# Attention and gated convolution on one core: row-tiled bf16 transposes for q and k, whole-head copies out of PSUM, and a last product split by rows

## The chip, the cores and the metric

The kernel runs on 1 core of one Trainium2 chip. The metric is the device time of one execution in microseconds (us).

PE is the matmul engine (TensorE), DVE is VectorE, ACT is ScalarE, POOL is GpSimd, SP issues DMAs. In this program PE, DVE and ACT each have a fixed order of instructions, so one that is late holds up those behind it (PE's wait of 3.45 us below is such a case).

## The reference, cut to what matters

```python
# q, k, v: (8 batches, 8 heads, 576 positions, 64), float32
scores = (q @ k.T) / 8, kept only where |i - j| <= 32
attn   = softmax(scores);  x = attn @ v, heads side by side: (8, 576, 512)
h      = relu(x @ w_in)                      # 512 -> 1024
conv   = three taps along the sequence, one weight per channel
out    = (h * sigmoid(conv)) @ w_out         # 1024 -> 512
```

Inputs and output are float32; the kernel computes in bf16. Scores are small (q and k are drawn with 0.1 deviation), so the weights within a window are nearly equal.

## The kernel before: the parts that matter

The kernel writes no instruction order by hand. A planner in Python takes operations with estimated costs, priorities and buffers, plays them on a model of the engines, and emits the result as a fixed order per engine. So each change of a cost, a buffer count or a rule may reorder the whole program.

q and k arrive with the head dimension along the free axis, and the scores need it on the partitions. A partition holds 9 neighbouring positions, so a turned row has position `r * 9 + j` (r: partition, j: 0 to 8). Nine 128x128 matmuls against the identity turn one pair of heads, and copies put the results in order:

```python
for n, js in enumerate(((0, 1, 2, 3), (4, 5, 6, 7), (8,))):
    ...
    tensor.matmul(ps.ap[:, x:x + 128], h.ap[:, j]..., ident, start=True, stop=True)   # float32 in PSUM
    ...
    if n < 2:                                  # 512 elements, written in runs of 4, 18 bytes apart
        o_ = to.ap[:, 2*y:2*y+2, PAD:PAD+S].rearrange("p x (r j) -> p x r j", j=RP)
        copier(e, o_[:, :, :, js[0]:js[0]+4], ps.ap.rearrange("p (j x r) -> p x r j", j=4, x=2))
if y == 1:                                     # j = 8 of q and k: 256 single elements, 18 bytes apart
    copier(e, o_[:, :, :, RP - 1], cs.ap[:, 0:256].rearrange("p (x r) -> p x r", x=4))
```

The middle tap of the convolution runs on PE for chunk 0 and on DVE for the others (`TAP(c, m): c > 0`), w_out is cast by POOL or DVE (`ENG1`), and the products with w_out come last in a chunk:

```python
def project(c, i, prio):                       # 12 chunks of 384 rows, 3 blocks of 128 rows each
    ...
    for m in range(MB):                        # 8 row blocks of w_out, one accumulation
        tensor.matmul(ps.ap, gT.ap[:, m, 128*i:128*i+128], w_out_sb[:, m, :], start=(m == 0), stop=(m == MB-1))
...
NHT = 4                                        # buffers for the convolution's input, per shape
NRING, NATTN, NGT, NQKB = 4, 3, 3, 8           # loads, weights of attention, gates, staged q and k
AHEAD = 2                                      # PSUM banks that attention must leave free
```

The softmax here doesn't subtract the row's maximum and nothing guards it: scores larger than these inputs give would overflow.

## Time and profile before

| | before |
|---|---|
| time, median of 3 | 273.63 us (271.94 to 273.75) |
| span of the profile | 268.6 us |
| PE / DVE / ACT busy | 89% / 82% / 77% |

These lines are from the profile's page: span, busy time by engine, PE's busy tenths and granted clock in 40 slices of 6.7 us (a 9 is 90% or more), and the chain of work that ended last, by engine.

```profile
span 268.6 us, 6936 instructions
PE 238.9 (89%) x2661; PEld 146.7 (55%) x2686; DVE 221.0 (82%) x522; ACT 206.3 (77%) x465; POOL 55.8 (21%) x80
PE   8799984669799899979999989979999999999974
PEclk9999998668999999999999999999999999999998
PE 49%; DVE 26%; ACT 19%; issue 4%; ACTq 0%; DVEq 0%
```

PE has a hole in the seventh to ninth slice, where the granted clock falls too. The chain is PE for only half of the span and runs through DVE and ACT for 45% of it. That is not all waiting time of PE, which is idle for 11% of the span. The windows view says what was busy around the hole (the first line names the columns; a figure in brackets is the number of instructions, and the last three are granted clock, DMA share and GB/s):

```profile
core 0: us, PE busy (x) PEld busy (x) DVE busy (x) ACT busy (x) POOL busy (x), PEclk, DMA share, GB/s
0.00:40.00 40.00, 34.97 (x440) 24.85 (x441) 33.38 (x108) 32.48 (x74) 4.71 (x26) 1.00 1.00 289
40.00:60.00 20.00, 11.78 (x153) 7.39 (x154) 18.37 (x44) 10.71 (x38) 8.97 (x9) 0.72 0.78 212
60.00:150.00 90.00, 83.34 (x989) 51.83 (x998) 79.48 (x176) 72.98 (x165) 33.00 (x36) 0.99 0.79 220
150.00:245.00 95.00, 90.50 (x992) 53.64 (x1002) 79.01 (x176) 78.44 (x166) 9.12 (x9) 1.00 0.17 53
```

From 40 to 60 us DVE is the busy one. Its timeline (start, duration, engine, operation, out<-in, count) shows four casts of w_out in one block, with the taps that PE needs behind them:

```profile
41.88 1.02 DVE L292 SCALAR_TENSOR_TENSOR gT<-tn,hT 128x384 bf16<-128x384 f32 x2
42.81 3.32 DVE L292 CAST w_out_sb<-st 128x512 bf16<-128x512 f32 x4
46.05 0.24 DVE L292 RECIPROCAL rec<-pf 128x4 f32<-128x4 f32 x2
46.21 0.38 DVE L292 SCALAR_TENSOR_TENSOR tn<-hT,conv_w_sb,pf 128x192 f32<-128x192 bf16 x1
```

PE's timeline of the same microseconds (in brackets the idle time before, and what ended it):

```profile
42.36 0.83 PE L292 MATMUL pf<-hT,diag_w 128*128 128x192 bf16 x8
46.64 1.34 PE L292 MATMUL pf<-qkT 64*128 64x64 bf16 x36 [3.45 <-DVE tn L292]
```

The copies of the turned q and k, from the groups by shape (busy us, mean ns of one, idle before):

```profile
L292 ACT CAST qkT<-pf 128x512 bf16<-128x512 f32 x45 | 33.2, 785 | 2.0 <-PE pf L292 2.0
L292 ACT CAST qkT<-pf 128x256 bf16<-128x256 f32 x13 | 17.7, 1359 | 0.0
L292 DVE CAST qkT<-pf 128x512 bf16<-128x512 f32 x19 | 13.6, 721 | 0.4 <-PE pf L292 0.3
L292 DVE CAST qkT<-pf 128x256 bf16<-128x256 f32 x3 | 3.9, 1294 | 0.0
```

Half as many elements take nearly twice as long in the 256-element form: the difference is how they are written. And PE's last matmuls, from its timeline; the last gate ends on DVE at 261.0 us:

```profile
258.33 0.49 PE L292 MATMUL pf<-hT,diag_w 128*128 128x384 bf16 x2 [0.74 <-ACT hT L292]
258.66 1.67 PE L292 MATMUL pf<-w_out_sb,gT 128*128 128x512 bf16 x6
261.07 3.84 PE L292 MATMUL pf<-w_out_sb,gT 128*128 128x512 bf16 x17 [0.74 <-DVE gT L292]
```

### The profile page before, as it was taken

The page shows a single profiled execution, that of the slowest core. Times are in us where ns is not written, and L with a number is a line of the kernel's source. Part 1 is how long each engine was busy: PE and PEld are TensorE (multiplying, and loading weights), DVE is VectorE, ACT ScalarE, POOL GpSimd, SP SyncE. Part 2 cuts the span into 40 slices and gives each one's busy share as a digit, 9 for nine tenths or more (in the row PEclk, how much of TensorE's full clock was granted, in tenths as well). Part 3 has the DMA queues.
Part 4 walks back from the last instruction along what each step waited for, and adds up shares of the span by engine and source line. Part 5 has one row for each costly group of instructions (what it writes and reads, how often), then busy time and mean ns, then how long its engine had stood idle before and what let it go on. Part 6 is the DMA issues. An engine that isn't in the chain of part 4 may idle for free.

```text
span 268.6 us, 6936 instructions
## 1 busy us (share of the span) xinstructions
PE 238.9 (89%) x2661; PEld 146.7 (55%) x2686; DVE 221.0 (82%) x522; ACT 206.3 (77%) x465; POOL 55.8 (21%) x80
## 2 busy tenths in 40 slices
PE   8799984669799899979999989979999999999974
PEld 5468653248565564454565655555656545655531
DVE  7998599976999988989798986987799878976640
ACT  3898994466796988796877998897787995776642
POOL 2002005601554535063021560130000000000000
PEclk9999998668999999999999999999999999999998
DMA  7999999654995999599911901101202111111213
GB/s 227 265 307 393 246 291 348 113 159 130 292 274 174 261 330 250 159 338 251 297 68 41 220 36 64 56 2 40 82 2 78 41 39 41 41 61 58 79 40 117
DMA packets 53573, 42.40 MB, mean 158 GB/s; under 512 B 38668, under 2 KB 38692, under 8 KB 53540
## 3 DMA queue, kind: packets, MB, share of 16 engines
q1 hardware_dynamic: 53504, 41.95, 54.4%
q8 instruction: 21, 0.34, 0.5%
q14 instruction: 12, 0.10, 0.1%
q10 hardware_dynamic: 36, 0.01, 0.1%
HBM read 32.52 MB, written 9.44 MB: 156 GB/s over the span
## 4 chain that ended last, share of the span: by engine, by line
PE 49%; DVE 26%; ACT 19%; issue 4%; ACTq 0%; DVEq 0%
PE pf L292 49%; ACT qkT L292 7%; DVE gT L292 6%; ACT tn L292 5%; DVE tn L292 4%; DVE attn L292 3%; ACT attn L292 3%; ACT hT L292 3%; DVE xn L292 2%; DVE qkT L292 2%; DVE w_out_sb L292 2%; DVE vo L292 2%; ACT xT L292 1%; DVE ve L292 1%; ACT y L292 1%
## 5 line engine op out<-in xcount | busy, mean ns | idle before, releaser
L292 PE MATMUL pf<-xT,w_in_sb 128*128 128x385 bf16 (+2 forms) x416 | 75.4, 316 | 1.7 <-ACT xT L292 1.0
L292 DVE SCALAR_TENSOR_TENSOR gT<-tn,hT 128x384 bf16<-128x384 f32 (+1 forms) x104 | 58.2, 577 | 15.9 <-ACT tn L292 14.9
L292 PE MATMUL pf<-w_out_sb,gT 128*128 128x512 bf16 x263 | 68.4, 393 | 2.8 <-DVE gT L292 0.7
L292 ACT ACTIVATE tn<-tn 128x384 f32<-128x384 f32 (+1 forms) x96 | 47.8, 523 | 20.1 <-DVE tn L292 19.7
L292 DVE SCALAR_TENSOR_TENSOR tn<-hT,conv_w_sb,pf 128x384 f32<-128x384 bf16 (+1 forms) x96 | 53.3, 575 | 10.4 <-PE pf L292 9.7
L292 ACT ACTIVATE hT<-pf 128x385 bf16<-128x385 f32 (+2 forms) x104 | 50.6, 521 | 8.9 <-PE pf L292 7.9
L292 PEld LDWEIGHTS <-w_in_sb 128*128 128x128 bf16 x416 | 38.9, 98 | 23.5 <-issue 2.2
L292 ACT CAST qkT<-pf 128x512 bf16<-128x512 f32 (+1 forms) x58 | 48.2, 914 | 2.0 <-PE pf L292 2.0
L292 PE MATMUL pf<-hT,diag_w 128*128 128x384 bf16 (+1 forms) x216 | 45.7, 315 | 4.3 <-ACT hT L292 3.1
L292 PEld LDWEIGHTS <-gT 128*128 128x128 bf16 x288 | 28.4, 100 | 33.2 <-issue 4.0
L292 ACT ACTIVATE attn<-pf 128x512 bf16<-128x512 f32 (+1 forms) x96 | 41.1, 538 | 0.4 <-PE pf L292 0.4
L292 POOL TENSOR_SCALAR qkb<-st 128x1152 bf16<-128x1152 f32 x24 | 31.1, 1300 | 46.4 <-DMA st<-in_q_dram 21.7
L292 ACT COPY y<-pf 128x512 f32<-128x512 f32 x35 | 20.8, 594 | 17.4 <-PE pf L292 17.3
L292 POOL TENSOR_SCALAR ve<-vst 128x512 bf16<-128x512 f32 x31 | 20.7, 687 | 49.9 <-PE pf L292 35.7
L292 DVE TENSOR_TENSOR attn<-attn,mask 128x1152 bf16<-128x1152 bf16 x32 | 25.7, 803 | 3.1 <-ACT attn L292 2.8
L292 DVE TENSOR_TENSOR xn<-pf,rec 128x256 bf16<-128x256 f32 x71 | 26.4, 410 | 0.2
L292 PEld LDWEIGHTS <-diag_w 128*128 128x128 bf16 x216 | 18.0, 97 | 14.8 <-issue 5.6
L292 PE MATMUL pf<-ident,qkb 128*128 128x128 bf16 x288 | 24.1, 222 | 2.1 <-DVE qkb L292 1.7
L292 PEld LDWEIGHTS <-qkb 128*128 128x128 bf16 x288 | 18.9, 99 | 7.0 <-DVE qkb L292 2.7
L292 PEld LDWEIGHTS <-qkT 64*128 64x128 bf16 x576 | 11.7, 96 | 17.0 <-issue 12.7
L292 PE MATMUL pf<-qkT 64*128 64x64 bf16 x576 | 15.1, 194 | 6.5 <-DVE tn L292 3.5
L292 PE MATMUL pf<-ve,attn 128*64 128x65 bf16 x384 | 17.2, 198 | 3.7 <-DVE attn L292 3.0
(43 smaller groups left out, 191.0 us busy)
## 6 DMA issues: line engine op xcount, KB each, us to landing
st<-in_q_dram SPq DMA_DIRECT2D x16, 576.0 KB, 6.1
st<-in_k_dram SPq DMA_DIRECT2D x16, 576.0 KB, 6.3
out_dram<-y SPq DMA_DIRECT2D x36, 256.0 KB, 2.0
vst<-in_v_dram SPq DMA_DIRECT2D x24, 256.0 KB, 8.1
vst<-in_v_dram SPq DMA_DIRECT2D x16, 192.0 KB, 4.6
st<-in_moe_w_in_dram SPq DMA_DIRECT2D x2, 1024.0 KB, 7.9
st<-in_moe_w_out_dram SPq DMA_DIRECT2D x2, 1024.0 KB, 7.9
conv_w<-in_moe_conv_w_dram ACTq DMA_DIRECT2D x1, 12.0 KB
```

Source lines behind the costliest of these rows:

```text
L292: return lambda *args, **kwargs: fixed(do(*args, **kwargs))
```

## The change

The intent: let two transposes run side by side in PE's two row halves, keep the turned values in bf16 so that a head's 576 positions fit one PSUM bank, copy a head out in one contiguous write, take load off DVE, and leave PE little to do after the last gate. The fit rests on what the Trainium skill states in "PSUM — Partial Sum Buffer", Specifications: a bank holds 2 KiB per partition, and a transpose writes its input's type while other matmuls write float32 (576 values are 1,152 bytes in bf16 and 2,304 in float32).

The core of the diff; cuts are marked with `...`, and what follows a `#` or stands in brackets is a note:

```diff
-    pf = Pool([psum.tile([128, 512], FP32, name=f"pf{i}") for i in range(8)])
+    pf = Banks(psum.tile([128, 4096], FP32, name="pf"))          # another choice among free banks
 ...
-        for n, js in enumerate(((0, 1, 2, 3), (4, 5, 6, 7), (8,))):
 ...  (the transposes and copies shown above)
+        turned = lambda x: ps[x].ap.bitcast(BF16)[:, 0:S]
+        for n, js in enumerate(((0, 1, 2, 3), (4, 5, 6, 7, 8))):
+            def emit(e, js=js):
+                for j in js:
+                    for x in range(2):
+                        tensor.transpose(
+                            turned(x)[:, 64 * j:64 * j + 64],
+                            h.ap[64 * x:64 * x + 64, j].rearrange("p e d -> p (e d)"),
+                            ident[64 * x:64 * x + 64, 64 * x:64 * x + 64],
+                        )
 ...
+            copier(e, to.ap[:, 2 * y + x, PAD:PAD + S].rearrange("p (r j) -> p r j", j=RP),
+                   turned(x).rearrange("p (j r) -> p r j", j=RP))
 ...
-    return c > 0
+    return c > TAP0                                               # TAP0 = 1
 ...
-    (tap: PSUM -> SBUF tile tn, tanh in place)
+    (tap: in place in PSUM, tanh PSUM -> tn)
 ...
-                cast_w("out", m, CASTWO + 0.1 * m, ENG1)           # POOL, DVE
+                cast_w("out", m, CASTWO + 0.1 * m, ENGW)           # POOL, ACT
 ...
+        cuts = (0, 3, 5, 6, 7, MB) if c == NCH - 1 else (0, MB)   # one operation per cut
-                project(c, i, 8.0 * (c + 1) + (PYAT[i] if c < NCH - 1 else 0.0))
+                project(c, i, 8.0 * (c + 1) + PYAT[i] if c < NCH - 1 else 8.0 * c + 3.6 + 0.1 * i)
 ...
-NHT = 4
-NRING, NATTN, NGT, NQKB = 4, 3, 3, 8
-AHEAD = 2
+NHT = 6
+NRING, NATTN, NGT, NQKB = 4, 3, 2, 6                              # and 5 tn, 3 y buffers
+AHEAD = 0
 ...
-        engines = ("SP", "PE", "ACT", "DVE", "POOL")
+        engines = ("SP", "PE", "POOL", "ACT", "DVE")              # who picks first, in the planner
 ...  (a blocked DVE or POOL operation no longer blocks those behind it, in the planner)
```

More of the change, by code (lines that the diff above doesn't have):

```diff
@@ L22, in __init__, with take, room, give @@
         self.free = [(-1.0, i) for i in range(len(bufs))]
+    def take(self, span):
+        if not self.free:
+            return None
+        self.free.sort()
+        return self.free.pop(0)[1]
+    def room(self, spans, spare):
+        return len(self.free) >= len(spans) + spare
+    def give(self, now, index, span):
+        self.free.append((now, index))
+    def ap(self, index, span):
+        return self.bufs[index]
+class Banks:
+    def __init__(self, tile_):
+        self.tile = tile_
+        self.free = {i: -1.0 for i in range(8)}
+    def runs(self, span):
+        return [i for i in range(9 - span) if all(i + k in self.free for k in range(span))]
+    def take(self, span):
+        if span == 1:
+            at = min(self.free, key=lambda i: (i < 3, self.free[i], -i))
+        else:
+            at = self.runs(span)[0]
+        for k in range(span):
+            del self.free[at + k]
+        return at
+    def room(self, spans, spare):
+        if len(self.free) < sum(spans) + spare:
+            return False
+        return all(s == 1 or self.runs(s) for s in spans)
+    def give(self, now, index, span):
+        for k in range(span):
+            self.free[index + k] = now
+    def ap(self, index, span):
+        return self.tile[:, 512 * index:512 * (index + span)]
 class Slot:
-    def __init__(self, pool):
-        self.pool, self.index, self.users = pool, None, 0
+    def __init__(self, pool, span=1):
+        self.pool, self.span, self.index, self.users = pool, span, None, 0
     @property
     def ap(self):
-        return self.pool.bufs[self.index]
+        return self.pool.ap(self.index, self.span)
 class Op:
@@ L87, in run @@
         mode = None
-        lock = {"DVE": 0.0, "POOL": 0.0}
+        lock = {"DVE": 0.0, "POOL": 0.0, "PE": 0.0}
         dma_free, rings = 0.0, []
@@ L121, in note @@
                 t, d = t + max(x, 1e-6), d - max(x, 1e-6)
-        late[0].free = [x for x in late[0].free if x[1] != late[1]]
+        late.take(1)
         push(filler_until, "free", late)
@@ L143, in run @@
                 elif kind == "free":
-                    x[0].free.append((now, x[1]))
+                    x.give(now, 7, 1)
                 elif kind == "done":
@@ L148, in run @@
                         if not s.users:
-                            s.pool.free.append((now, s.index))
+                            s.pool.give(now, s.index, s.span)
                     for n in x.after:
@@ L158, in run @@
                 while free[e] <= now + 1e-9:
-                    best = None
+                    best, blocked = None, False
+                    other = {"DVE": "POOL", "POOL": "DVE"}.get(e, "PE")
                     for o in todo[e]:
@@ L162, in run @@
                             continue
-                        short = False
+                        if o.two and lock[other] > now + 1e-9:
+                            blocked = True
+                            continue
                         need = {}
                         for s in o.acquire:
-                            need[s.pool] = need.get(s.pool, 0) + 1
-                        for p, n in need.items():
-                            if len(p.free) < n + (o.spare if p is self.psum else 0):
-                                short = True
-                        if short:
+                            need.setdefault(s.pool, []).append(s.span)
+                        if not all(p.room(n, o.spare if p is self.psum else 0) for p, n in need.items()):
                             continue
@@ L178, in run @@
                     if best is None:
+                        if blocked:
+                            free[e] = lock[other]
+                            push(free[e], "look", e)
                         if e == "PE" and now < filler_until:
@@ L187, in run @@
                     t = now
-                    if e in lock and o.two:
-                        other = "POOL" if e == "DVE" else "DVE"
-                        if lock[other] > now + 1e-9:
-                            free[e] = lock[other]
-                            push(free[e], "look", e)
-                            break
                     gone.add(o)
@@ L196, in run @@
                     for s in o.acquire:
-                        s.pool.free.sort()
-                        s.index = s.pool.free.pop(0)[1]
+                        s.index = s.pool.take(s.span)
                     out.append((t, len(out), e, o))
@@ L224, in run @@
                         free[e] = now + occ
-                        if e in lock and o.two:
+                        if o.two and e in lock:
                             lock[e] = now + occ
@@ L228, in run @@
                     push(free[e], "look", e)
+                    o.fin = done
                     push(done + self.LATENCY[e if e == "SP" else "ACT"], "done", o)
@@ L236 @@
 FILL = 23.0
-NHT = 4
-NRING, NATTN, NGT, NQKB = 4, 3, 3, 8
+NHT = 6
+NTN, NQKT, NY = 5, 3, 3
+NRING, NATTN, NGT, NQKB = 4, 3, 2, 6
 LOADV1, LOADWO, CASTWO = -89.0, -89.5, 6.0
+TN_SBUF = True
+MASKER = ("DVE",)
+ENGW = ("POOL", "ACT")
 ENG1 = ("POOL", "DVE")
-AHEAD = 2
+TAP0 = 1
+AHEAD = 0
 PLACE = {0: (-30.0, -10.0), 1: (1.0, 9.0), 2: (11.0, 21.0), 3: (21.0, 31.0), 4: (34.0, 46.0),
@@ L304 @@
     qkb = pool("qkb", NQKB, [128, RP, 2, 64], BF16)
-    qkT = pool("qkT", 3, [128, 4, W], BF16)
+    qkT = pool("qkT", NQKT, [128, 4, W], BF16)
     ve_b = [sb.tile([128, NBLK, H, 65], BF16, name=f"ve{i}") for i in range(2)]
@@ L313 @@
     gT_p = pool("gT", NGT, [128, MB, CH], BF16)
-    tn_p = pool("tn", 4, [128, CH], FP32)
-    y_p = pool("y", 4, [128, d_model], FP32)
+    tn_p = pool("tn", NTN, [128, CH], FP32) if TN_SBUF else None
+    y_p = pool("y", NY, [128, d_model], FP32)
     w_in_sb = sb.tile([128, KC, d_ff], BF16, name="w_in_sb")
@@ L378, with masker @@
     op = pl.op
+    def masker(b):
+        costs = {"DVE": c_dve(1152, 2.0), "POOL": c_pool(1152, 2.6)}
+        return {e: costs[e] for e in (("DVE",) if b < 2 else MASKER)}
     def copier(e, out_, in_):
@@ L507, in transposes @@
             qkT_slot[b, i] = Slot(qkT)
-            c_slot[b, i] = Slot(pf)
-        to, cs = qkT_slot[b, i], c_slot[b, i]
+        to, ps = qkT_slot[b, i], [Slot(pf), Slot(pf)]
         parts = 2 if ("qkb", b, i, y, 1) in pl.writer else 1
-        for n, js in enumerate(((0, 1, 2, 3), (4, 5, 6, 7), (8,))):
-            ps = cs if n == 2 else Slot(pf)
-            reads = [("qkb", b, i, y, 0)] if n == 0 or parts == 1 else [("qkb", b, i, y, 1)]
-            def emit(e, js=js, n=n, ps=ps):
-                for z, j in enumerate(js):
-                    x = 128 * z + (128 * y if n == 2 else 0)
-                    tensor.matmul(
-                        ps.ap[:, x:x + 128], h.ap[:, j].rearrange("p e d -> p (e d)"),
-                        ident, start=True, stop=True,
-                    )
-            first = y == 0 and n == 0
-            acq = ([ps] if n < 2 or y == 0 else []) + ([to] if first else [])
-            o = op(f"tr {'qk'[y]}{b}{i}.{n}", {"PE": 0.0575 * len(js)}, emit, prio, reads=reads + ["ident"],
-                   writes=[("ptr", b, i, y, n)], acquire=acq, behind=None if first else leader["tr", b, i, n == 2],
-                   use=[h] + ([ps] if n == 2 else []), spare=ahead)
-            if first:
-                leader["tr", b, i, False] = leader["tr", b, i, True] = o
-            elif n == 2 and y == 0:
-                leader["tr", b, i, True] = o
-            if n < 2:
-                def emit(e, js=js, ps=ps):
-                    o_ = to.ap[:, 2 * y:2 * y + 2, PAD:PAD + S].rearrange("p x (r j) -> p x r j", j=RP)
-                    copier(e, o_[:, :, :, js[0]:js[0] + 4],
-                           ps.ap.rearrange("p (j x r) -> p x r j", j=4, x=2))
-                op(f"ev {'qk'[y]}{b}{i}.{n}", evac_cost(512), emit, prio + 0.05, reads=[("ptr", b, i, y, n)],
-                   writes=[("qkT", b, i, y, n)], use=[ps, to])
@@ L538, in transposes @@
-        if y == 1:
-            def emit(e):
-                o_ = to.ap[:, :, PAD:PAD + S].rearrange("p x (r j) -> p x r j", j=RP)
-                copier(e, o_[:, :, :, RP - 1], cs.ap[:, 0:256].rearrange("p (x r) -> p x r", x=4))
-            op(f"ev 8{b}{i}", evac_cost(256), emit, prio + 0.05, reads=[("ptr", b, i, y, 2) for y in range(2)],
-               writes=[("qkT", b, i, 2)], use=[cs, to])
+        turned = lambda x: ps[x].ap.bitcast(BF16)[:, 0:S]
[8 more added lines that the diff above has]
+                        )
+            o = op(f"tr {'qk'[y]}{b}{i}.{n}", {"PE": 0.03 * len(js)}, emit, prio, mode="row",
+                   reads=[("qkb", b, i, y, min(n, parts - 1)), "ident"], writes=[("ptr", b, i, y, n)],
+                   acquire=(ps if n == 0 else []) + ([to] if y + n == 0 else []),
+                   behind=leader.get(("tr", b, i, y)), use=[h] + ps, spare=ahead)
+            leader["tr", b, i, y] = o
@@ new lines, in transposes, with emit_ev @@
+        if y == 0:
+            leader["tr", b, i, 1] = o
+        def emit_ev(e, x):
+            copier(e, to.ap[:, 2 * y + x, PAD:PAD + S].rearrange("p (r j) -> p r j", j=RP),
+                   turned(x).rearrange("p (j r) -> p r j", j=RP))
+        for x in range(2):
+            op(f"ev {'qk'[y]}{b}{i}.{x}", evac_cost(S), lambda e, x=x: emit_ev(e, x),
+               prio + 0.05, reads=[("ptr", b, i, y, n) for n in range(2)], writes=[("qkT", b, i, y, x)],
+               use=[ps[x], to])
@@ L551, in scores @@
         for x in range(2):
-            tiles = [Slot(pf), Slot(pf), Slot(pf)]
+            ps = [Slot(pf), Slot(pf), Slot(pf)]
             lists = [[(x, e, t) for t in range(8)] for e in range(2)]
@@ L558, in scores, with emit @@
                     todo += lists[e][n:n + 1]
-            def emit(e_, x=x, tiles=tiles, todo=todo):
+            def emit(e_, x=x, ps=ps, todo=todo):
                 for x_, e, t in todo:
@@ L563, in emit @@
                     tensor.matmul(
-                        tiles[n // 512].ap[:, n % 512:n % 512 + 64],
+                        ps[n // 512].ap[:, n % 512:n % 512 + 64],
                         to.ap[64 * e:64 * e + 64, 2 + x_, 64 * t:64 * t + 128],
@@ L570, in scores, with emit_exp @@
                f"sc {b}{i}{x}", {"PE": 0.28}, emit, prio + 0.001 * x, mode="row",
-               reads=[("qkT", b, i, y, n) for y in range(2) for n in range(2)] + [("qkT", b, i, 2)],
+               reads=[("qkT", b, i, y, x0) for y in range(2) for x0 in range(2)],
                behind=leader["sc", b, i, 0] if x else None,
-               writes=[("sc", b, i, x)], acquire=tiles + ([at_] if x == 0 else []),
+               writes=[("sc", b, i, x)], acquire=ps + ([at_] if x == 0 else []),
                use=[to], spare=ahead)
-            for e in range(3):
-                n = (512, 512, 128)[e]
-                c0 = 1152 * x + 512 * e
-                def emit_exp(e_, e=e, n=n, c0=c0, tiles=tiles):
-                    scalar.activation(at_.ap[:, c0:c0 + n], tiles[e].ap[:, 0:n], AF.Exp, bias=0.0, scale=scale)
-                op(f"exp {b}{i}{x}{e}", {"ACT": c_act(n)}, emit_exp, prio + 0.1,
-                   reads=[("sc", b, i, x)], writes=[("exp", b, i, x, e)], use=[tiles[e], at_])
+            for n, (c0, c1) in enumerate(((0, 512), (512, 1024), (1024, 1152))):
+                def emit_exp(e_, x=x, c0=c0, c1=c1, ps=ps[n]):
+                    scalar.activation(
+                        at_.ap[:, 1152 * x + c0:1152 * x + c1], ps.ap[:, 0:c1 - c0], AF.Exp, bias=0.0, scale=scale
+                    )
+                op(f"exp {b}{i}{x}{n}", {"ACT": c_act(c1 - c0)}, emit_exp, prio + 0.1,
+                   reads=[("sc", b, i, x)], writes=[("exp", b, i, x, n)], use=[ps[n], at_])
             def emit_mask(e_, x=x):
-                vector.tensor_tensor(
+                (vector if e_ == "DVE" else gpsimd).tensor_tensor(
                     out=at_.ap[:, 1152 * x:1152 * x + 1152], in0=at_.ap[:, 1152 * x:1152 * x + 1152],
@@ L589, in emit_mask @@
                 )
-            op(f"mask {b}{i}{x}", {"DVE": c_dve(1152, 2.0)}, emit_mask, prio + 0.15, two=True,
-               reads=[("exp", b, i, x, e) for e in range(3)], writes=[("attn", b, i, x)], use=[at_])
+            op(f"mask {b}{i}{x}", masker(b), emit_mask, prio + 0.15, two=True,
+               reads=[("exp", b, i, x, n) for n in range(3)], writes=[("attn", b, i, x)], use=[at_])
     def values(b, i, c, prio, ahead, engines):
@@ L677, in unit @@
         touched = sorted({(s // S, s % S // 128) for s in range(lo, hi)})
-        ps, pc, tn = Slot(pf), Slot(pf), Slot(tn_p)
+        ps, pc = Slot(pf), Slot(pf)
         hT = Slot(hT_p[shape])
@@ L730, in emit_tap, with emit_tanh @@
                 vector.scalar_tensor_tensor(
-                    out=in3(tn.ap), in0=taps(1), scalar=conv_w_sb[:, 1, m:m + 1], in1=in3(pc.ap),
+                    out=in3(pc.ap), in0=taps(1), scalar=conv_w_sb[:, 1, m:m + 1], in1=in3(pc.ap),
                     op0=ALU.mult, op1=ALU.add,
                 )
-            op(f"tap {u}", {"DVE": c_dve(nc_)}, emit_tap, prio + 0.55, reads=[("pc", u), "conv_w"], writes=[("tap", u)],
-               acquire=[tn], use=[pc, hT])
-            def emit_tanh(e_):
-                scalar.activation(tn.ap[:, 0:nc_], tn.ap[:, 0:nc_], AF.Tanh, bias=0.0, scale=1.0)
-            op(f"tanh {u}", {"ACT": c_act(nc_, sbuf=True)}, emit_tanh, prio + 0.6, reads=[("tap", u)],
-               writes=[("tanh", u)], use=[tn])
-        else:
-            def emit_tanh(e_):
-                scalar.activation(tn.ap[:, 0:nc_], pc.ap[:, 0:nc_], AF.Tanh, bias=0.0, scale=1.0)
-            op(f"tanh {u}", {"ACT": c_act(nc_)}, emit_tanh, prio + 0.6, reads=[("pc", u)],
-               writes=[("tanh", u)], acquire=[tn], use=[pc])
+            op(f"tap {u}", {"DVE": c_dve(nc_ + 58)}, emit_tap, prio + 0.55, reads=[("pc", u), "conv_w"], writes=[("tap", u)],
+               use=[pc, hT])
+        tn = Slot(tn_p) if TN_SBUF else pc
+        def emit_tanh(e_):
+            scalar.activation(tn.ap[:, 0:nc_], pc.ap[:, 0:nc_], AF.Tanh, bias=0.0, scale=1.0)
+        op(f"tanh {u}", {"ACT": c_act(nc_)}, emit_tanh, prio + 0.6, reads=[("tap" if on_dve else "pc", u)],
+           writes=[("tanh", u)], use=[pc], acquire=[tn] if TN_SBUF else [])
         def emit_gate(e_):
@@ L753, in unit @@
         op(f"gate {u}", {"DVE": c_dve(nc_)}, emit_gate, prio + 0.7, reads=[("tanh", u)], writes=[("g", c, m, part)],
-           use=[tn, hT, gT], two=True)
+           use=[tn, hT, gT], two=TN_SBUF)
     out_rows = out.rearrange("b s f -> (b s) f")
@@ L760, in project, with emit @@
         parts = [p for p in (None, 0, 1) if ("g", c, 0, p) in pl.writer]
-        def emit(e_):
-            for m in range(MB):
-                tensor.matmul(
-                    ps.ap, gT.ap[:, m, 128 * i:128 * i + 128], w_out_sb[:, m, :], start=(m == 0), stop=(m == MB - 1),
-                )
         if len(parts) == 2:
             parts = [0] if 128 * i + 128 <= HW else [1] if 128 * i >= HW else parts
-        op(f"py {c}{i}", {"PE": MB * 0.2158}, emit, prio, acquire=[ps], use=[gT], writes=[("py", c, i)],
-           reads=[("g", c, m, p) for m in range(MB) for p in parts] + [("w_out", m) for m in range(MB)])
+        cuts = (0, 3, 5, 6, 7, MB) if c == NCH - 1 else (0, MB)
+        for n, (m0, m1) in enumerate(zip(cuts, cuts[1:])):
+            def emit(e_, m0=m0, m1=m1):
+                for m in range(m0, m1):
+                    tensor.matmul(
+                        ps.ap, gT.ap[:, m, 128 * i:128 * i + 128], w_out_sb[:, m, :],
+                        start=(m == 0), stop=(m == MB - 1),
+                    )
+            leader["py", c, i] = op(
+                f"py {c}{i}.{n}", {"PE": (m1 - m0) * 0.2158}, emit, prio + (n if c == NCH - 1 else 0),
+                acquire=[ps] if n == 0 else [], use=[gT, ps], writes=[("py", c, i, n)],
+                behind=leader.get(("py", c, i)),
+                reads=[("g", c, m, p) for m in range(m0, m1) for p in parts] + [("w_out", m) for m in range(m0, m1)])
         def emit_y(e_):
             copier(e_, y_sb.ap, ps.ap)
-        op(f"y {c}{i}", evac_cost(d_model), emit_y, prio + 0.2, reads=[("py", c, i)], writes=[("y", c, i)],
+        op(f"y {c}{i}", evac_cost(d_model), emit_y, prio + 0.2, reads=[("py", c, i, n) for n in range(len(cuts) - 1)],
+           writes=[("y", c, i)],
            acquire=[y_sb], use=[ps])
@@ L864 @@
             for i in range(3):
-                project(c, i, 8.0 * (c + 1) + (PYAT[i] if c < NCH - 1 else 0.0))
-    order = pl.run(START, (0.107, "filler"), FILL, (pf, 7))
+                project(c, i, 8.0 * (c + 1) + PYAT[i] if c < NCH - 1 else 8.0 * c + 3.6 + 0.1 * i)
+    order = pl.run(START, (0.107, "filler"), FILL, pf)
     order.sort(key=lambda x: (x[0], x[1]))
-    dummy = pf.bufs[7]
+    dummy = pf.ap(7, 1)
     for t, _, e, o in order:
```

## The prediction

> **What bounds it now.** The page gives PE 89% busy, DVE 82%, ACT 77%; the chain that ended last is PE 49%, DVE 26%, ACT 19%. The timeline's starts tell more of PE: a 512-column product takes 216 ns from start to start, a 385-column one 164, a 128x128 transpose 56, a row-tiled 64-column score about 17. Over all matmuls that is about 205 of 268.6 us (estimate). The rest: 118 mode changes (a full matmul before a row-tiled one takes 259 instead of 164 ns: about 12 us), half clock (7 us), waits (some 30 us). The worst stage is 40 to 60 us: in the windows view PE is busy 11.8 of 20 us, DVE 18.4, granted clock 0.72. DVE's timeline shows four w_out casts in one block of 3.3 us, taps behind them, and PE's longest wait (3.5 us, on DVE's tap). From 60 us on PE is mostly 93 to 99% busy.
>
> **What changes.**
> - Transposes: 288 of 56 ns (16.1 us) become 576 row-tiled ones of 64 columns, shaped like the scores: 17 ns each, 10 us. But mode changes go from 118 to 158: +4 us. The Trainium skill, "TensorEngine Tiling (Array Packing)", Key Properties, says that changing the tiling mode drains the array; this trace's 0.1 us agrees. Chunk 1's third tap adds 1.3 us. PE's work hardly falls.
> - Copies out: now 80, ACT 45x785 + 13x1359 ns = 50.9 us, DVE 17.5. The 1359 ns form has 256 elements but writes single ones with gaps: gaps cost. Afterwards 64 copies of 576, written contiguously. Contiguous xT copies of 512 took 631 (ACT) and 685 ns (DVE), so about 690 and 750: ACT 35 -> 24 us, DVE 29 -> 22.
> - DVE also loses w_out casts (4.4), chunk 1 taps (6.4), casts of q, k, v, w_in (9.6 us), to POOL and ACT. Taps now write PSUM: some 50 ns more on 80. In all ACT about -28 us, DVE -15, POOL +13.
> - Tail: after the last gate PE does 17 products (3.7 us); afterwards 3 (0.65). But the others only move ahead of that gate, where PE is idle for 1.8 us, and three copies and stores come together: -0.5 to -1.5 us.
>
> **On the critical path.** The engines relieved are mostly not the limit after 60 us: 43 us of ACT and DVE time buy perhaps 4 to 5 us of short waits there. The gain is the stage at 40 to 60 us: 8 to 9 us of PE wait and 2 to 3 us of half clock. With tail 1 and PE 0 to 1: about 16 us.
>
> **Predicted:** 257.5 us, 8 in 10 between 250 and 266. Faster by over 2%: 0.92; within 2%: 0.07; slower: 0.01.
>
> **What would show it right.** Copies near 0.7 us; ACT near 178 us busy, DVE 206; no half clock after 20 us, no PE wait over 2 us on the tap; transposes near 17 ns start to start; gain mostly before 65 us; last three products 0.7 us after the last gate.
>
> **What would make it wrong.** Strided bf16 reads of PSUM as slow as strided writes (ACT gains nothing); transposes not overlapping (27 ns: +6 us); transposes not counted as activity (the skill's "TensorE: Matmul & The Clock Gate", Part 4, says this; no run shows it yet), so half clock stays; DMA, busy 0.8 to 1.1 until 140 us, becoming the next limit; two gT buffers in place of three stalling gates.

## The result, and the profile after

| | before | changed |
|---|---|---|
| first measurement, median (range, runs) | 272.78 (271.12 to 273.75, 4) | 256.47 (251.65 to 329.01, 4) |
| measured again, median (range, runs) | 271.28 (268.05 to 273.43, 11) | 252.72 (252.13 to 254.27, 6) |
| ratio, first and again | | 0.9254 [0.9154, 0.9353], 0.9351 [0.9300, 0.9402] |

A ratio is the mean time of one kernel's runs over that of the other's of the same rounds, so it is not quite the ratio of the medians. The change takes 6.5 to 7.5% less time. Two of the four first runs of the changed kernel were slow (329.01 and 260.06 us), and so its first ratio rests on two.

The only profile of the first measurement fell in the slower of these: 329 us at a granted clock of 0.757. No other run of any kernel showed that clock, so nothing is concluded from it, and the profile after is the fast one taken again. Its page:

```profile
span 251.2 us, 7589 instructions
PE 234.3 (93%) x3002; PEld 139.7 (56%) x3002; DVE 212.0 (84%) x488; ACT 183.4 (73%) x437; POOL 73.0 (29%) x107
PE   7799999699699999999799999999899999999981
PEclk9999999979999999999999999999999999999999
PE 72%; DVE 18%; ACT 5%; issue 3%; POOL 1%; ACTq 0%; DVEq 0%; POOLq 0%
```

PE is now 72% of the chain that ended last, where it was 49%; ACT fell from 19% to 5%. The windows:

```profile
0.00:40.00 40.00, 36.90 (x558) 25.75 (x560) 31.13 (x95) 30.27 (x75) 20.54 (x51) 1.00 1.01 288
40.00:60.00 20.00, 17.42 (x298) 12.62 (x298) 15.84 (x42) 15.92 (x50) 10.90 (x13) 0.91 0.94 264
60.00:150.00 90.00, 85.69 (x1166) 49.62 (x1163) 86.24 (x176) 69.81 (x163) 36.31 (x38) 1.00 0.79 222
150.00:245.00 95.00, 93.44 (x993) 51.51 (x987) 77.51 (x176) 66.22 (x150) 5.25 (x7) 1.00 0.14 51
```

From 40 to 60 us PE is busy 17.4 instead of 11.8 us. But later stages gained too: 83.3 to 85.7 and 90.5 to 93.4. The copies are now 64, near 0.7 us each:

```profile
L343 ACT COPY qkT<-pf 128x576 bf16<-128x576 bf16 x35 | 23.1, 686 | 1.4 <-PE pf L343 1.4
L343 DVE COPY qkT<-pf 128x576 bf16<-128x576 bf16 x29 | 21.4, 751 | 0.6 <-PE pf L343 0.6
```

PE's end; the last gate ends at 245.7 us:

```profile
243.08 0.49 PE L343 MATMUL pf<-hT,diag_w 128*128 128x384 bf16 x2 [0.71 <-ACT hT L343]
243.40 1.47 PE L343 MATMUL pf<-w_out_sb,gT 128*128 128x512 bf16 x6
245.76 0.82 PE L343 MATMUL pf<-w_out_sb,gT 128*128 128x512 bf16 x3 [0.89 <-DVE gT L343]
```

### Where the time went: one scale for all kernels

Windows in microseconds compare unlike things once two kernels have drifted apart. So I also counted finished work. Each relu, exponential, reciprocal, gate, copy of x and copy of y in the trace counts as the PE time of the matmuls whose result it takes (at the start-to-start times that the prediction names; 184.3 us in every kernel, with the transposes of q and k left out), and it counts as done when the relu, copy and so on starts. The table gives the time at which 20, 100 and 170 us of that work were done.

| kernel (its profile) | 20 | 100 | 170 | end |
|---|---|---|---|---|
| before | 62.7 | 167.7 | 250.2 | 268.6 |
| changed | 53.3 | 153.3 | 231.8 | 251.2 |
| difference | -9.4 | -14.4 | -18.4 | -17.4 |

So 9.4 us come before the first mark and 9.0 between the first and the last, and 1.0 us is lost at the end. The same traces give PE's own account: the work at its start-to-start times with 0.1 us per mode change, the time added by half clock, and the rest, which is waiting (the 1.2 us before the first matmul included, and what the filler matmuls of the first 8 us lose, which take 213 ns each there and 109 afterwards, in both kernels). The trace of before lacks 25 matmul records; its work is taken from an experiment with the same matmuls in the same order and no record missing.

| stretch of work | kernel | time | PE work | half clock | waiting |
|---|---|---|---|---|---|
| 0 to 20 | before | 62.7 | 40.0 | 4.9 | 17.8 |
| | changed | 53.3 | 41.4 | 1.9 | 10.0 |
| 20 to 170 | before | 187.5 | 172.1 | 0 | 15.4 |
| | changed | 178.5 | 171.0 | 0 | 7.5 |

PE has as much to do as before; it waits less, in equal parts early and late, 7.8 and 7.9 us.

### The profile page after: what moved, and what is told of

Its sections match the earlier page's. It is cut to its first block, busy times and chain, and to the rows that moved or that the text cites. A ratio compares the mean times of both kernels' runs of the same rounds, so it can differ in the third digit from the quotient of the medians.

```text
span 327.0 us, 7565 instructions
## 1 busy us (share of the span) xinstructions
PE 315.8 (97%) x2978; PEld 166.4 (51%) x3002; DVE 216.5 (66%) x488; ACT 189.7 (58%) x437; POOL 70.6 (22%) x107
## 4 chain that ended last, share of the span: by engine, by line
PE 92%; DVE 3%; issue 2%; ACT 1%; POOL 0%; ACTq 0%; POOLq 0%
PE pf L343 92%; DVE diag_w L343 1%; DVE qkT L343 0%; ACT y L343 0%; DVE mask L343 0%; ACT tn L343 0%; DVE rec L343 0%; DVE xn L343 0%; DVE pf L343 0%; DVE gT L343 0%; POOL mask L343 0%; ACT hT L343 0%; DVE ve L343 0%; POOL hT L343 0%; POOL ident masks.py:199 0%
## 5 line engine op out<-in xcount | busy, mean ns | idle before, releaser
L343 PE MATMUL pf<-xT,w_in_sb 128*128 128x385 bf16 (+2 forms) x416 | 104.7, 410 | 0.3 <-DVE xn L343 0.3
L343 PE MATMUL pf<-w_out_sb,gT 128*128 128x512 bf16 x264 | 94.8, 511 | 3.4 <-issue 1.4
L343 DVE SCALAR_TENSOR_TENSOR pf<-hT,conv_w_sb,pf 128x384 f32<-128x384 bf16 x80 | 48.6, 619 | 41.6 <-PE pf L343 32.4
L343 DVE SCALAR_TENSOR_TENSOR gT<-tn,hT 128x384 bf16<-128x384 f32 (+1 forms) x104 | 58.7, 582 | 21.2 <-ACT tn L343 20.7
L343 PE MATMUL pf<-hT,diag_w 128*128 128x384 bf16 (+1 forms) x232 | 63.1, 395 | 0.7 <-ACT hT L343 0.6
L343 ACT ACTIVATE tn<-pf 128x384 f32<-128x384 f32 (+1 forms) x104 | 47.7, 478 | 18.0 <-DVE pf L343 13.7
L343 POOL TENSOR_SCALAR qkb<-st 128x1152 bf16<-128x1152 f32 (+2 forms) x32 | 37.0, 1159 | 95.4 <-PE pf L343 60.0
L343 ACT COPY y<-pf 128x512 f32<-128x512 f32 x34 | 19.9, 585 | 56.0 <-PE pf L343 53.3
L343 DVE COPY qkT<-pf 128x576 bf16<-128x576 bf16 x29 | 21.5, 753 | 9.4 <-PE pf L343 9.3
L343 ACT COPY qkT<-pf 128x576 bf16<-128x576 bf16 x35 | 22.1, 650 | 3.5 <-PE pf L343 3.4
L343 PE MATMUL pf<-zero 128*128 128x256 bf16 x112 | 22.2, 360 | 1.3 <-DVE zero L343 1.3
L343 PEld LDWEIGHTS <-attn 128*64 128x64 bf16 x640 | 14.1, 121 | 10.0 <-issue 6.9
L343 PEld LDWEIGHTS <-qkT 64*128 64x128 bf16 x576 | 12.4, 100 | 12.5 <-issue 10.8
```

The lines of the kernel that those rows point to most:

```text
L343: return lambda *args, **kwargs: fixed(do(*args, **kwargs))
```

## The experiments

The theory was the stage theory: most of the gain is DVE's relief at 40 to 60 us. The rival was the copy theory: cheaper copies of the turned q and k shorten waits everywhere. Further candidates were PE's shorter transposes, and the tail. All 12 runs gave outputs that pass the comparison.

### The change again

No edit.

> The changed kernel again, because its only profile fell in a state with a granted clock of 0.757 (327 us). Expected: 250 to 258 us and a ratio near 0.925; in a fast profile, by my theory (the gain is the stage at 40 to 60 us), more than half of the 20 us gain lies before 65 us, PE waits nowhere over 2 us on the tap, and the clock is full from about 15 us on. By the rival (cheaper copies of the turned q and k shorten waits everywhere) the gain is spread evenly, about 1 us per 13 us of span. A repeat of 0.75 clock in other rounds would say that the state belongs to this kernel more than to the kernel before.

Measured: 252.72 us, ratio 0.9351; six runs, all fast. 9.4 of 17.4 us (54%) came before the first mark, at 53 against 63 us, so "more than half" holds, barely. The longest wait of PE that names the tap is gone. What stays is one window of half clock at 49 to 53 us, where the prediction had expected none.

### DVE's relief alone

```diff
 (the kernel before)
-    return c > 0
+    return c > 1
-                cast_w("out", m, CASTWO + 0.1 * m, ENG1)
+                cast_w("out", m, CASTWO + 0.1 * m, ("POOL", "ACT"))
```

> The kernel before with only VectorE's relief at 40 to 60 us: w_out cast by POOL and ACT, and chunk 1's middle tap on PE. Stage theory: 8 to 11 us faster (ratio 0.96 to 0.97), the 3.5 us wait of PE on the tap gone, no half clock after 20 us. Copy theory: 2 to 4 us faster at most, since the copies of q and k stay as they were.

Measured: 264.65 us (263.71 to 265.84), ratio 0.9783 [0.9719, 0.9846]: 6.6 us, between what the two theories expected. By the marks (58.2, 162.8, 245.3, end 263.6) it gains 4.5 us by the first and only 0.4 us more by the third. The wait of 3.5 us on the tap is gone, but PE then waits 2.9 us for masked attention weights from DVE, until 49.7 us: the stage had a second wait behind the first. One window of half clock stays too (51.9 to 55.3 us), which the stage theory had not expected.

```profile
49.69 0.22 PE L292 MATMUL pf<-ve,attn 128*64 128x65 bf16 x1 [2.89 <-DVE attn L292]
```

### The new transposes and copies alone

```diff
 (the kernel before)
 the part of the diff with `turned`, and the scores' list of what they read; nothing else
```

> The kernel before with only the new transposes and their contiguous copies (mode changes 118 to 171). Stage theory: 3 to 6 us faster (ratio 0.98 to 0.99), the gap at 43 us stays. Copy theory: 10 to 14 us faster (ratio 0.95 to 0.965). If mode changes eat it: 0 to 2 us.

Measured: 256.75 us (255.45 to 258.55), ratio 0.9493 [0.9421, 0.9565]: 14.5 us, over twice what the relief gives. The stage theory had expected 3 to 6. By the marks (58.7, 156.1, 235.8, end 254.1) 4.0 us come early and 10.4 between the first and the last, although mode changes went from 118 to 171. The stage theory falls as the main cause. PE's own work is not the gain either: 288 transposes of 56 ns became 576 of 15.6 (7 us less), but 53 more mode changes of 0.1 us cost 5.

### The tail alone

```diff
 (the kernel before)
 the part of the diff with `cuts`, and the last chunk's priority; nothing else
```

> The kernel before with only the last chunk's products split by rows of w_out. Expected 0.5 to 1.5 us faster (ratio 0.994 to 0.998): PE has 3 instead of 17 products after the last gate, but the others displace work of the last units. If PE were mostly idle there: 3 us (0.989).

Measured: 272.54 us, ratio 1.0079 [1.0014, 1.0144]: 0.8% slower by the ratio, 1.3 us by the medians: in any case not faster. From the third mark to the end it takes 19.4 us against 18.4 of before. PE's timeline shows why:

```profile
259.69 0.81 PE L292 MATMUL pf<-hT,diag_w 128*128 128x384 bf16 x4
260.34 0.82 PE L292 MATMUL pf<-xT,w_in_sb 128*128 128x385 bf16 x4
261.91 0.49 PE L292 MATMUL pf<-hT,diag_w 128*128 128x384 bf16 x2 [0.74 <-ACT hT L292]
262.23 1.50 PE L292 MATMUL pf<-w_out_sb,gT 128*128 128x512 bf16 x6
264.64 0.82 PE L292 MATMUL pf<-w_out_sb,gT 128*128 128x512 bf16 x3 [0.91 <-DVE gT L292]
```

Only 3 products follow the last gate, as meant. But the products that moved went in front of the last unit's matmuls, so its last taps start at 261.91 instead of 258.33 us, and the waits of 0.74 and 0.91 us are still there. Behind them three copies and three stores come at once: from the end of the last copy of y to the end of the span it is 3.9 us instead of 3.0.

### Dense copies, nothing else

```diff
 (the kernel before; the result is wrong on purpose)
-                    o_ = to.ap[:, 2 * y:2 * y + 2, PAD:PAD + S].rearrange("p x (r j) -> p x r j", j=RP)
-                    copier(e, o_[:, :, :, js[0]:js[0] + 4], ...)
+                    o_ = to.ap[:, 2 * y:2 * y + 2, PAD + 64 * js[0]:PAD + 64 * js[0] + 256]
+                    copier(e, o_.rearrange("p x (r j) -> p x r j", j=4), ...)
-                copier(e, o_[:, :, :, RP - 1], ...)
+                copier(e, to.ap[:, :, PAD + S - 64:PAD + S], ...)
```

> The kernel before with the same 80 copies of the turned q and k, same sizes, same order on every engine, but written densely into wrong places, so the result is wrong on purpose; PE's transposes stay as they were. Copy theory: ACT's 58 copies fall from 51 to about 35 us and DVE's from 17.5 to about 14.5 us, and the kernel gets 7 to 12 us faster (ratio 0.955 to 0.975), most of what the new transposes and copies gave alone (14 us). If the gain came from PE's shorter transposes: 0 to 3 us.

Measured: 265.45 us (262.44 to 266.35), ratio 0.9785 [0.9698, 0.9872]: 5.8 us, a little under the copy theory's range and above the rival's. The groups by shape:

```profile
L292 ACT CAST qkT<-pf 128x512 bf16<-128x512 f32 x45 | 25.9, 612 | 2.8 <-PE pf L292 2.8
L292 ACT CAST qkT<-pf 128x256 bf16<-128x256 f32 x13 | 5.3, 406 | 0.0
```

Same elements, same count, same place in every engine's order: 785 became 612 ns and 1359 became 406. Neighbouring instructions on ACT overlap (the next one starts 0.13 us before a dense copy of 512 ends, and 0.57 us before one of 256 single elements does), so durations must not be summed: the time in which ACT or DVE ran such a copy, overlaps counted once, fell from 65.6 to 44.1 us. Between the first and the last mark the time fell by 5.8 us with PE's work unchanged, so these are waits of PE that went. The cost of gaps in the writes is shown, and so is its price for the kernel before: about 6 us (8 in a second measurement below) where the new transposes and copies (b_turn) gained 14.5.

### New transposes, but copies with gaps

```diff
 (the kernel before with the new transposes; order on every engine unchanged)
-            copier(e, to.ap[...].rearrange("p (r j) -> p r j", j=RP), turned(x).rearrange("p (j r) -> p r j", j=RP))
+            for j0, j1 in ((0, 4), (4, 9)):
+                copier(e, o_[:, :, j0:j1], i_[:, :, j0:j1])
```

> The kernel before with the new transposes, in the same order on every engine, but each copy of 576 split in two that write runs of 4 and 5 elements with gaps, as the old copies did. Copy theory: a pair takes about 1.2 to 1.4 us instead of 0.65 to 0.75, and the kernel falls back to 267 to 274 us. If PE's transposes made the gain: 257 to 260 us.

Measured: 260.4 us (258.48 to 264.12), ratio 0.9594: 3.7 us slower than with one contiguous copy, where the copy theory had expected at least 10. But that forecast supposed 1.2 to 1.4 us a pair. The two copies of a pair took 0.50 and 0.53 us on ACT:

```profile
L292 ACT COPY qkT<-pf 128x320 bf16<-128x320 bf16 x43 | 22.6, 526 | 0.0
L292 ACT COPY qkT<-pf 128x256 bf16<-128x256 bf16 x43 | 21.3, 496 | 1.2 <-PE pf L292 1.2
```

They overlap. In the trace the shorter one runs first and the other starts 0.29 us after it, and where work stands ready the next instruction starts 0.63 us after the pair's start, against 0.53 us for the single copy of b_turn. With overlaps counted once, ACT and DVE ran these copies for 49.3 us here, 42.1 in b_turn and 65.6 in the kernel before. So the edit added 7 us of copying and not the 29 us or more that the forecast implied (64 pairs, 0.45 us or more each): most of what the new copies had saved stayed saved, and so did 10.8 of the 14.5 us. By the marks (62.3, 160.4, 240.3) the loss lies almost wholly before the first; between the first and the last it takes 178.0 us against 177.1 of b_turn and 187.5 of before.

This run is therefore a weak test, which neither refutes the copy theory nor confirms it. What speaks against its plain form, "time of copies turns into time", is the dense experiment: it takes nearly as much off the copies (65.6 to 44.1 us) as the new transposes do (to 42.1), for less of the gain (6 to 8 of 14.5 us). Where the rest of b_turn's gain comes from no run isolates: its copies are also fewer (64 in place of 80), the scores wait for other pieces, and the planner gives another order.

### New transposes, one row tile after the other

```diff
 (the kernel before with the new transposes)
-                for j in js:
-                    for x in range(2):
+                for x in range(2):
+                    for j in js:
```

> The kernel before with the new transposes and copies, but the two row tiles one after the other and not in turns, so that two transposes don't overlap. I expect 27 to 30 ns from start to start instead of 17 to 21, about 5 us more on PE. Copy theory: 1 to 4 us slower than with turns (258 to 261 us). If PE's transposes made the gain: 5 us or more slower (262 us).

Measured: 260.38 us (258.66 to 262.0), ratio 0.9637. The mean distance between starts of neighbouring transposes was 18.3 ns against 15.6 with turns, not 27 to 30 (22.5 and 21.0 if six pauses of 0.2 to 0.8 us within the groups of each run, which are waits, are counted in). That is about 1.5 us over 576 transposes. Its loss of 3.6 us against b_turn also lies before the first mark (61.9 against 58.7), with half clock from 45.5 to 59.2 us instead of 45.0 to 55.2. So this edit did not do what it was meant to, and says only that taking row tiles in turns matters little to PE. Both this run and the one with gaps had 13.7 us of half clock in the early stage against 10.2 of b_turn, so up to 1.7 us of the loss of each (an estimate: half of the 3.4 us more) is the clock; what set it off no run shows.

### Relief and new transposes together

```diff
 both edits above, nothing else of the change
```

> The kernel before with VectorE's relief and with the new transposes, and nothing else of the change (old bank choice, old planner rules, old buffer counts, old tail, taps written to SBUF). If the two parts add: 271.3 - 14.5 - 6.6 = 250 us, as fast as or faster than the whole change (252.7), and the rest of the change is worth nothing or less. If the rest matters: 254 us or more.

Measured: 262.31 us (259.25 to 263.99), ratio 0.9651. Not 250: it is slower than the new transposes alone. The parts do not add. Its profile is of the fastest run (span 257.4 us) and keeps up with the changed kernel to the second mark (154.7 against 153.3); then PE waits 2.0 us for a relu at 214 us, half clock follows for 3.4 us, and 5.6 us are lost by the third mark. The slower runs were not profiled.

### The same with the change's buffer counts

```diff
 (relief and new transposes)
-NHT = 4
-NRING, NATTN, NGT, NQKB = 4, 3, 3, 8
-AHEAD = 2
+NHT = 6
+NRING, NATTN, NGT, NQKB = 4, 3, 2, 6
+AHEAD = 0
```

> The kernel before with VectorE's relief, the new transposes, and the change's buffer counts (6 conv inputs, 2 gate buffers, 6 staged q and k, no spare banks), but the old planner rules, old tail and taps written to SBUF. If the counts are what relief and transposes alone lacked (262 us): 252 to 255 us. If the planner's rules or the taps' place are: 259 to 264 us.

Measured: 254.13 us (249.94 to 255.95), ratio 0.9259 [0.9184, 0.9334], which rests on two runs only; the other four are over 1.5% above the fastest, at nearly the same clock (0.986 to 0.993 against 0.992 to 0.997). All six lie well below 262. So four numbers are worth some 8 us here, and with them two parts of the change reach the whole change (252.7 us). The planner's new rules, the bank choice and the taps' place add nothing that these times can show. Which of the four numbers it is stays open, and so does the share of the relief: the new transposes with these counts and without the relief were not run, nor the counts alone.

### The short copies dense, the long ones with gaps

```diff
 (the kernel before; wrong on purpose)
-                    o_ = to.ap[:, 2 * y:2 * y + 2, PAD:PAD + S].rearrange("p x (r j) -> p x r j", j=RP)
+                    o_ = to.ap[:, 2 * y:2 * y + 2, PAD:PAD + S - 64].rearrange("p x (r j) -> p x r j", j=RP - 1)
 and the short copies as in the dense experiment
```

> The kernel before where only the 16 short copies (256 elements, 1.36 us, single elements with gaps) are written densely, into wrong places (wrong on purpose); the 64 copies of 512 keep runs of 4 with gaps. Lump theory (a few long copies, each the last thing that the scores wait for, hold up everything behind them): the short copies fall to 0.41 us and nearly all of the 6 us that the dense copies gave comes back (ratio 0.977 to 0.985). Sum theory (the total of copy time counts): those 16 are 15 of the 24 us saved there, so about 3.5 us (0.987).

Measured: 263.16 us, ratio 0.9678 [0.9625, 0.9730]. But the experiment failed as a test: its runs of 4 elements stand 16 bytes apart (a row of 8) instead of 18, and at that distance the gaps cost nothing. Its profile (of a slow run, but this is ACT's own duration):

```profile
L292 ACT CAST qkT<-pf 128x512 bf16<-128x512 f32 x45 | 25.8, 610 | 2.6 <-PE pf L292 2.6
```

610 ns is the dense time. So this is a second measurement of dense copies, 8.3 us of medians after 5.8, and whether the few long copies or the sum did it stays open. What it adds points to the reason: not the gap as such but where the runs start.

### A tail that fills waits only

```diff
 (the change)
-        cuts = (0, 3, 5, 6, 7, MB) if c == NCH - 1 else (0, MB)
+        cuts = tuple(range(MB + 1)) if c == NCH - 1 else (0, MB)
-                f"py {c}{i}.{n}", ..., emit, prio + (n if c == NCH - 1 else 0),
+                f"py {c}{i}.{n}", ..., emit, prio,
-                project(c, i, ... else 8.0 * c + 3.6 + 0.1 * i)
+                project(c, i, ... else 8.0 * c + 7.6 + 0.1 * i)
```

> The whole change, but the last chunk's products one by one and with a priority behind the last unit's own matmuls, so that they fill its waits and don't delay its gate. The change's tail cost about 1 us (end minus the point where 170 us of work are done: 19.4 against 18.4 us of before). Expected: last gate about 3 us earlier, some 10 products after it, 1.5 to 2.5 us faster than the change (250.2 to 251.2 us).

Measured: 252.39 us (250.45 to 253.87), ratio 0.9303 against 0.9351 of the change in other rounds. In the profile the tail after the third mark is 16.5 us, against 19.4 of the change and 18.4 of before. PE's timeline has no wait left in it:

```profile
239.65 1.03 PE L343 MATMUL pf<-w_out_sb,gT 128*128 128x512 bf16 x4
240.53 0.48 PE L343 MATMUL pf<-hT,diag_w 128*128 128x384 bf16 x2
240.85 4.49 PE L343 MATMUL pf<-w_out_sb,gT 128*128 128x512 bf16 x20
```

The tail is 2.9 us shorter, as expected or more; the total moved by 0.3 us of medians or 1.3 us by the ratios, less than expected and within the scatter. The mechanism is shown, its size in the total is not.

### Fewer mode changes

```diff
 (the kernel of the tail above)
-    SWITCH = 0.1
+    SWITCH = 0.8
```

> The same, with the planner's price of a mode change at 0.8 instead of 0.1, which leaves 135 instead of 158 changes. If each costs 0.1 us on a busy PE: 2.3 us faster than the run beside it; if waiting for the grouping costs as much: the same or slower.

Measured: 246.79 us (244.46 to 247.65), ratio 0.9080 [0.9027, 0.9133], beside 252.39 in the same rounds: 5.6 us faster, over twice the expected 2.3. Between the first and the last mark it takes 174.6 us against 178.7: PE's work fell from 171.0 to 168.8 us (the mode changes), its waits from 7.7 to 5.8. Grouping row-tiled work saved waits as well; why, no run shows. This version beats both kernels, and its result is right.

```profile
span 245.1 us, 7583 instructions
PE 232.3 (95%) x3002; PEld 139.6 (57%) x3002; DVE 209.7 (86%) x484; ACT 184.8 (75%) x441; POOL 73.0 (30%) x107
```

## Why the prediction was right or wrong, point by point

The time was right: 257.5 us with 250 to 266 predicted, 256.5 measured first and 252.7 again; about 16 us of gain predicted, 17.4 in the profile. The sum held better than its terms, and that is partly luck: the later waits gave some 3.4 us more than forecast and the tail 2 us less.

- **PE's work hardly falls: right.** 212.1 us became 212.4 over both stretches. The transposes took about 15 ns from start to start (17 predicted): two in different row halves start 3 ns apart and the next two 26 ns later, so they do run side by side. That is about 9 us in place of 16; 40 more mode changes of 0.1 us took much of that back.
- **Half clock and waits at 40 to 60 us: right in kind and size.** Waits before the first mark fell by 7.8 us (8 to 9 predicted) and half clock by 3.0 (2 to 3). The relief alone gave only 4.5 us there; the new transposes gave 4.0 of their own.
- **"43 us of ACT and DVE time buy perhaps 4 to 5 us of short waits there": the mis-sized term.** The relief was smaller (ACT 23 and DVE 9 us less busy) and bought more: waits between the first and the last mark fell by 7.9 us. The prediction took PE for "mostly 93 to 99% busy" from 60 us on; the windows have 91% at 60 to 80, 86% at 100 to 120 and 91% at 160 to 180 us, and the account above has 15.4 us of waiting there to be won. The new transposes alone took 10.4 us off that stretch. "Gain mostly before 65 us" was therefore half true (9.4 of 17.4).
- **The tail, -0.5 to -1.5 us: wrong sign.** It cost 1.0 us. The prediction had named the reason, that the products only move ahead of the last gate, but took the 1.8 us of idle time as filled. The moved products went before the last unit's matmuls and not into the waits.
- **"No half clock after 20 us": wrong.** One 3.4 us window remained at 49 to 53 us.
- **Copies near 0.7 us: right** (686 and 751 ns). ACT 178 predicted, 183 measured; DVE 206 and 212. Strided bf16 reads of PSUM are not slow. Taps into PSUM took 617 instead of 607 ns.
- **Two gate buffers as a risk: not seen.** The four counts together (two gate buffers, more convolution inputs, fewer staged q and k, no reserved banks) were what relief and transposes together needed: 262 to 254 us. Two gate buffers alone were not run.

What stays open: why relief and transposes with the old counts lose to transposes alone; which count matters, and whether the relief is still worth anything beside the counts; whether a few long copies or the sum of copy time held PE up; where the 6 to 9 us of b_turn's gain come from that dense copies alone don't give; and whether transposes count as activity for the clock, which the skill's "TensorE: Matmul & The Clock Gate", Part 4, denies and no run here tested.

## What to carry to other kernels

Where an order is planned from cost estimates, a part's worth is only defined beside the other parts: measure parts alone, together, and with the buffer counts retuned, before saying which of them did it. Before an experiment is read, check in its trace that the edit changed the cost that it was to change, with overlapping instructions counted once. Write 2-byte results in whole contiguous rows and put the stride on the PSUM read. Work that is split off to shorten a tail must stand behind the last chain's own work, or it lengthens that chain; and where PE is the limit, price mode changes higher than their own 0.1 us and look again.

## What the Trainium skill lacked or had wrong

- "SBUF — State Buffer", the note on cachelines in the section on the DMA port swizzle, says that accesses within one 16-byte line are fast and that crossing to a new line costs. The runs agree and give sizes that the page lacks, for ACT writes of bf16: a copy with runs of 4 at an 18-byte step lasts 785 ns per 512 elements against 612 dense, about 1.4 ns per run (173 ns over 128 runs); single elements at 18 bytes last 1359 against 406 ns per 256, about 3.7 ns each; runs of 4 at a 16-byte step cost nothing (610 ns), though each begins a new 16 bytes. From start to start with work standing ready the cost is smaller: 598 against 478 ns and 784 against 264.
- "PSUM — Partial Sum Buffer", Specifications, warns that non-contiguous patterns slow matmuls, and says nothing of ACT and DVE reads. Reading bf16 at a step of 128 bytes, with contiguous writes, took 686 ns (ACT) and 751 ns (DVE) for 576 elements, in line with the copies of x in the same run, which read 512 float32 values contiguously (602 and 686 ns).
- "TensorEngine Tiling (Array Packing)", Key Properties, says that a mode change drains the array, without a size. In these traces it is about 0.1 us: a 385-column matmul is followed after 164 ns by its like and after 259 ns by a row-tiled one.
- "TensorE: Matmul & The Clock Gate", Part 1, gives about 25 ns as the least distance between starts however small the matmul. In the experiment with one row tile after the other, the 64-column transposes of one row tile, in blocks of four or five, have recorded starts 17.6 ns apart on average (8 to 30 ns singly).
- No page says what the clock of 0.757 over a whole execution on one core is, seen in one run of the changed kernel (329 us) and in no other run.
